# A fused window attention with two gated MLPs on one core: three chunks per output bank, later output weights and integer additions on VectorE in one stage

## The chip, the core and the metric

The kernel runs on one core of a Trainium2 chip. The engines are named as the profile names them: PE (TensorE, the matrix engine; PEld is its weight load), DVE (VectorE), ACT (ScalarE), POOL (GpSimd) and SP (the engine that issues the DMAs here). SBUF is the on-chip memory, PSUM the memory that PE writes its sums to. The metric is the time of one execution on the device, in microseconds; lower is better.

## What is computed

Window attention over four sequences of 576 tokens gives 2304 tokens of 512 numbers. Two gated MLPs follow, each with two input matrices of 512 x 1536 and an output matrix of 1536 x 512. The weights come as float64, and the kernel rebuilds float32 words from them itself. The part that matters here is the second MLP.

```python
x = attn_out.transpose(0, 2, 1, 3).reshape(B * S, H * D)      # 2304 x 512
gate = 1.0 / (1.0 + np.exp(-(x @ w_gate)))                    # first MLP
x = (gate * (x @ w_val)) @ w_out
a = x @ w_a                                                   # second MLP
b = x @ w_b
out = (a * b) @ w_out
```

## The kernel before

**Stages.** Attention comes first and runs on beside the first MLP of tokens 0 to 1279, up to about 341 us of the profiled execution. Then comes the stage of the change, to about 565 us: the second MLP of tokens 256 to 1279. A seam of some 27 us finishes its output and prepares the next operands; after it both MLPs of the last 1024 tokens run to the end.

**A quad.** The hidden width of 1536 is worked off in twelve chunks of 128 (NF = 12). For the 1024 tokens and one chunk, `quad` computes both products with seven matrix products instead of eight (line 846, six matmuls of 512 columns each, in PSUM tiles qa, qb and qc). ACT copies interim sums out (line 865), DVE adds them (line 868) and multiplies a by b (line 878, first qa, at the end qc), and DVE and ACT split the result into a high and a low part (lines 470 and 472). The second half of the hidden values lies in a buffer that `seconds` picks: one of its own, or one of the rings of the weights wa and wb.

**Output banks.** The output rows are eight PSUM banks of 128 x 512 (`row_banks`, `bank_sum`, tile accq, line 984). After every second chunk (PAIR = 2) eight jobs are put into the list `rest`: six matmuls per bank, three for each chunk, and then an addition into an SBUF sum on DVE (line 988); the first group is copied by ACT (line 986). `fill` takes jobs out of the list between the products of later quads. Two PSUM buffers serve these banks. The 256 tokens of block 0 are done on the side for six chunks in this stage (ALONE, `hidden`, line 461, and `projection`, line 514), and for three more in the seam.

**Decoding.** A weight matrix of a chunk (a, b or o for the output) is loaded from HBM into `stage` (three buffers). `decode_words` makes of it: low and ex on ACT (lines 374 and 377), a shift and a mask-and-or on DVE (lines 380 and 383), and the integer addition `wi + low` on POOL (line 387). `decode_pair` multiplies (line 393, DVE), rounds to the high part (line 399, ACT) and subtracts for the low part (line 402: DVE for a and b, POOL for o). Once a and b of a chunk are there, `combining` makes their four combinations, each with two POOL operations and a copy on ACT (lines 439, 441 and 442). The list `order` gives the sequence of the matrices: a, b and o of a chunk, then the next chunk. `need` drives it until a chunk is `ready`, which here happens with its o; `step_decode` takes single steps between the products of a quad. The ring of the output weights wo has four buffers.

**What sets the order.** The program is recorded in this sequence; then a scheduler, which has durations of its own, places the instructions on each engine. Each engine works its list off in order, so an instruction that waits holds up all that stand behind it on that engine.

Of the kernel before, what the change touches and what calls it, by code (L numbers as in the profile page):

```python
# [21 lines left out]
def tile_window_attention_gated_mlps(ctx, tc, q, k, v, w1g, w1v, w1o, w2a, w2b, w2o, out):  # L22
# [346 lines left out]
    def decode_words(F, i, nm):  # L369
        st = staged.pop((F, nm))  # L370
        w0, w1 = st[:, :, 0], st[:, :, 1]
        k = 3 * F + i if F > NF + 2 else 0
# [14 lines left out]
        nc.gpsimd.tensor_tensor(out=wi, in0=wi, in1=low, op=ALU.add)  # L387
# [249 lines left out]
    order = [(F, i, nm) for F in range(DECODED, NW) for i, nm in enumerate("abo")]  # L637
# [3 lines left out]
    def begin_matrix():  # L641
        if begun[0] == 0:
            load_weights(DECODED)
        if begun[0] < len(order):
            F, i, nm = m = order[begun[0]]
            begun[0] += 1
            since = len(nc.cur_bb.bb.instructions)
            whole(decode_words(*m))
            if F == NF + 2 and held[0]:
                for i in nc.cur_bb.bb.instructions[since:]:  # L650
                    tc.add_manual_dep(
                        i, held[0],
                        mybir.DependencyInfo(mybir.DependencyClass.NoSync, mybir.DependencyReason.DATA), reason="held",
                    )
            pending.append(m)
            if F + 1 < NW:
                load_matrix(F + 1, nm)

    def step_decode(turn):
# [17 lines left out]
        if nm == "o":  # L677
            ready[F] = parts[F]
        elif nm == "b" and F >= NF:
            combined_by.append(combining(F))  # L680
        return True
# [9 lines left out]
    def need(F, turn):  # L691
        while F not in ready:
            assert step_decode(turn), (F, turn)
# [409 lines left out]
    def row_banks(res, hs, rows, begin, end):  # L1103
# [3 lines left out]
        for i in range(2 * NP):  # L1107
# [19 lines left out]
    PAIR = 2  # L1127
# [11 lines left out]
    for fc in range(NF):  # L1139
        alone = ALONE.get(fc, ())  # L1140
        for i, f0 in enumerate(alone):
# [4 lines left out]
            if i == len(alone) - 1:  # L1146
                rest.append(lambda a=(1, 0, h0s, fc == 0, False): projection(*a))
# [9 lines left out]
        counts = ((0, 0, 1, 1, 1, 1, 0), (0, 0, 1, 1, 1, 1, 0)) if len(rest) <= 4 else ((0, 1, 1, 1, 1, 1, 1), (0, 1, 1, 1, 1, 1, 1))  # L1157
        extra = max(0, len(rest) - sum(counts[0]))

        def between(i):  # L1160
            fill(counts[0][i] + (extra if i == 4 else 0))
# [3 lines left out]
        hs.append((w["o"], quad(1, w, x_ops, between, g, seconds[fc % 3], lambda: None)))  # L1165
        if len(hs) == PAIR:
            fill(len(rest))
            row_banks(res, hs, (3 * N, N), fc == PAIR - 1, fc == NF - 1)
            hs = []
# [158 lines left out]
```

## Time and profile before

| what | us |
|---|---|
| runs before, median (lowest to highest of 3) | 965.94 (965.51 to 966.07) |
| the profiled execution | 966.96 |
| span of its trace | 965.1 |
| PE busy in the span | 927.0 (96%) |
| DVE busy | 705.4 (73%) |
| ACT busy | 480.0 (50%) |
| POOL busy | 358.7 (37%) |

A busy share is a mean over the whole span. PE is nearly always busy, and the stretches in which it isn't lie in the first 60 us and between 300 and 600 us. What a change in that second part is worth is read from the stretch itself: how long PE stands still there, and for whom.

### The profile page before, as it was taken

What the parts mean: (1) busy time and instruction counts of PE and PEld (TensorE: products, weight loads), DVE (VectorE), ACT (ScalarE), POOL (GpSimd) and SP (SyncE); (2) the same over time, 40 slices, a digit from 0 to 9 for tenths busy, and PEclk for the clock granted to TensorE, in tenths of its full rate; (3) what the DMA queues carried; (4) which work ended last, traced back from release to release, by engine and by line L of the source; (5) the groups of instructions that cost most, each with busy time, mean ns of one, the idle gap of its engine ahead of it and who ended that gap; (6) DMA issues with size and microseconds to landing.
All of it is one profiled execution on the core that took longest, in us unless ns stands there. A gap on an engine that the chain in (4) does not pass through costs nothing.

```text
span 965.1 us, 15642 instructions
## 1 busy us (share of the span) xinstructions
PE 927.0 (96%) x5504; PEld 772.7 (80%) x5504; DVE 705.4 (73%) x1343; ACT 480.0 (50%) x1063; POOL 358.7 (37%) x357
## 2 busy tenths in 40 slices
PE   7899999999999988899999998999999999999998
PEld 6798888888887766787777886788888888888886
DVE  7997877876567899967979576778888673354545
ACT  7887555677635456564645334654454233211111
POOL 4443232343248738855758217644440000000000
PEclk9999999999999999999999999999999999999999
DMA  8987698997478637763765547345456675554312
GB/s 213 247 238 222 217 316 287 336 292 239 138 235 287 218 131 233 257 210 130 251 231 195 196 151 254 117 160 168 135 173 199 217 254 159 167 168 129 102 66 87
DMA packets 144684, 193.68 MB, mean 201 GB/s; under 512 B 63584, under 2 KB 98912, under 8 KB 143968
## 3 DMA queue, kind: packets, MB, share of 16 engines
q1 hardware_dynamic: 144608, 192.71, 61.6%
q8 instruction: 43, 0.70, 0.3%
q14 instruction: 33, 0.27, 0.1%
HBM read 118.75 MB, written 69.47 MB: 195 GB/s over the span
## 4 chain that ended last, share of the span: by engine, by line
PE 48%; DVE 9%; POOL 3%; DMA 3%; issue 2%; ACT 1%; DVEq 0%; POOLq 0%; ACTq 0%
PE qa L846 16%; PE accq L984 11%; PE qb L846 8%; PE qc L846 4%; PE accy L947 3%; PE accx L947 2%; DVE wi L380 1%; DMA st_a<-in_moe_w_a_dram 1%; DVE ex L393 1%; POOL s L439 1%; DVE wi L383 1%; POOL wq L442 1%; PE gps L461 1%; PE vps L461 1%; PE acc L514 1%
## 5 line engine op out<-in xcount | busy, mean ns | idle before, releaser
L387 POOL TENSOR_TENSOR wi<-wi,low 128x512 int32<-128x512 int32 x72 | 103.9, 1443 | 144.2 <-DVE wi L383 109.6
L865 ACT ACTIVATE r<-qa 128x512 f32<-128x512 f32 x108 | 63.6, 596 | 107.6 <-PE qa L846 93.6
L442 POOL TENSOR_TENSOR wq<-s,wq 128x256 fp32r<-128x256 f32 x96 | 86.5, 907 | 73.7 <-ACT wq L441 72.3
L846 PE MATMUL qa<-op,wq 128*128 128x512 f32 x432 | 112.9, 389 | 0.4 <-ACT r L865 0.4
L846 PE MATMUL qb<-op,wq 128*128 128x512 f32 x432 | 111.1, 389 | 0.9 <-DVE qc L868 0.9
L461 PE MATMUL gps<-xh,wa 128*128 128x256 f32 (+1 forms) x392 | 104.9, 338 | 1.5 <-DVE h L472 1.0
L461 PE MATMUL vps<-xh,wb 128*128 128x256 f32 (+1 forms) x392 | 105.3, 337 | 0.8 <-ACT hr L485 0.8
L846 PEld LDWEIGHTS qb<-op,wq 128*128 128x128 f32 x432 | 81.0, 188 | 18.1 <-DVE qc L868 1.3
L846 PEld LDWEIGHTS qa<-op,wq 128*128 128x128 f32 x432 | 80.9, 188 | 17.3 <-ACT r L865 0.6
L562 PE MATMUL accm<-hh,wo 128*128 128x512 f32 (+1 forms) x296 | 87.3, 362 | 3.3 <-DVE gacc L539 1.9
L461 PEld LDWEIGHTS gps<-xh,wa 128*128 128x128 f32 x392 | 68.6, 189 | 11.4 <-DVE h L472 1.5
L461 PEld LDWEIGHTS vps<-xh,wb 128*128 128x128 f32 x392 | 68.9, 189 | 8.7 <-ACT hr L485 1.0
L984 PE MATMUL accq<-wo,h 128*128 128x512 f32 (+1 forms) x300 | 71.7, 382 | 2.8 <-DVE resf L988 2.7
L393 DVE SCALAR_TENSOR_TENSOR ex<-ex,wi 128x512 f32<-128x512 f32 x72 | 59.7, 829 | 17.7 <-POOL wi L387 10.3
L984 PEld LDWEIGHTS accq<-wo,h 128*128 128x128 f32 x300 | 54.9, 188 | 14.9 <-DVE resf L988 3.8
L461 PE MATMUL gps<-xl,wa 128*128 128x256 f32 (+1 forms) x196 | 65.6, 335 | 0.6 <-DVE xl L237 0.6
L470 ACT ACTIVATE hh<-qa 128x512 fp32r<-128x512 f32 x36 | 21.6, 599 | 89.0 <-DVE qa L878 60.0
L461 PE MATMUL vps<-xl,wb 128*128 128x256 f32 (+1 forms) x196 | 65.6, 335 | 0.0
L562 PEld LDWEIGHTS accm<-hh,wo 128*128 128x128 f32 x296 | 54.1, 193 | 13.8 <-DVE gacc L539 4.4
L984 PE MATMUL accq<-wo,hh 128*128 128x512 f32 x184 | 55.7, 394 | 4.9 <-ACT hh L470 3.7
L846 PE MATMUL qa<-op,wa 128*128 128x512 f32 x216 | 55.7, 391 | 3.3 <-DVE g L868 3.3
L846 PE MATMUL qa<-op,wb 128*128 128x512 f32 x216 | 55.3, 391 | 2.4 <-ACT r L865 2.4
(177 smaller groups left out, 2114.9 us busy)
## 6 DMA issues: line engine op xcount, KB each, us to landing
wo<-ko SPq DMA_DIRECT2D x27, 512.0 KB, 3.9
wa<-ka SPq DMA_DIRECT2D x27, 512.0 KB, 4.6
st_o<-in_moe_w_out_dram SPq DMA_DIRECT2D x24, 512.0 KB, 4.9
ka<-wa SPq DMA_DIRECT2D x24, 512.0 KB, 5.1
kb<-wb SPq DMA_DIRECT2D x24, 512.0 KB, 4.1
ko<-wo SPq DMA_DIRECT2D x24, 512.0 KB, 4.0
kq<-wq SPq DMA_DIRECT2D x48, 256.0 KB, 3.2
wq<-kq SPq DMA_DIRECT2D x48, 256.0 KB, 3.2
```

The lines of the kernel that those rows point to most:

```text
L380: nc.vector.tensor_scalar(out=wi, in0=w1, scalar1=3, scalar2=(1 << 30) - 1, op0=ALU.logical_shift_left, op1=ALU.bitwise_and)
L383: nc.vector.scalar_tensor_tensor(out=wi, in0=w1, scalar=-(1 << 30), in1=wi, op0=ALU.bitwise_and, op1=ALU.bitwise_or)
L387: nc.gpsimd.tensor_tensor(out=wi, in0=wi, in1=low, op=ALU.add)
L393: nc.vector.scalar_tensor_tensor(out=wf, in0=wf, scalar=SMALLEST, in1=wi.bitcast(F32), op0=ALU.is_ge, op1=ALU.mult)
L442: nc.gpsimd.tensor_tensor(out=t[:, 1], in0=s, in1=t[:, 0].bitcast(F32), op=ALU.subtract)
L461: nc.tensor.matmul(ps, lhsT=a[:, c * P:(c + 1) * P], rhs=b[:, c, :], start=(n == 0), stop=(n == 3 * NP - 1))
L470: nc.scalar.activation(out=hh, in_=hr, func=AF.Copy, scale=factor)
L562: nc.tensor.matmul(ps[:, m], lhsT=a[:, sl], rhs=b, start=k == 0, stop=k == total - 1)
L846: nc.tensor.matmul(ps, lhsT=a[:, c * P:(c + 1) * P], rhs=b[:, c, :], start=first and n == 0, stop=n == 5, skip_group_check=True,)
L865: nc.scalar.activation(out=r[n], in_=ps, func=AF.Copy)
L947: nc.tensor.matmul(bank[k], lhsT=a[n][i][:, sl], rhs=b[n][j], start=start and m == 0, stop=m == 2, skip_group_check=True,)
L984: nc.tensor.matmul(ps, lhsT=a, rhs=b, start=n == 0, stop=n == len(pairs) - 1)
```

## The change

It has four parts, all in the stage from 341 to 565 us or just ahead of it.

- Output banks are formed after every third chunk (THREE): nine matmuls a bank instead of six, and four groups of eight additions instead of six. `row_banks` takes the banks that use the second halves of the hidden values first (`turned`).
- `order` brings the o of a chunk after the a and b of the next one, from chunk 3 on. A chunk is `ready` with its combinations, and whoever needs the o asks for it by name; loads run three matrices ahead in the same list as before.
- The addition `wi + low` of all matrices of the second MLP is issued on DVE instead of POOL.
- The slots between products take four jobs of the list per quad, whatever its length.

```diff
-        k = 3 * F + i if F > NF + 2 else 0
+        k = order.index((F, i, nm)) if F > NF + 2 else 0
...
-        nc.gpsimd.tensor_tensor(out=wi, in0=wi, in1=low, op=ALU.add)
+        (nc.vector if F >= NF else nc.gpsimd).tensor_tensor(out=wi, in0=wi, in1=low, op=ALU.add)
...
-    order = [(F, i, nm) for F in range(DECODED, NW) for i, nm in enumerate("abo")]
+    order = [(F, i, nm) for F in range(DECODED, NF + 2) for i, nm in enumerate("abo")]
+    for F in range(NF + 2, NW):
+        order += [(F, 0, "a"), (F, 1, "b")] + ([(F - 1, 2, "o")] if F > NF + 2 else [])
+    order.append((NW - 1, 2, "o"))
...
-            if F + 1 < NW:
-                load_matrix(F + 1, nm)
+            if at + 3 < len(order):
+                load_matrix(*order[at + 3][::2])
...
-        if nm == "o":
+        if nm == "o" and F < NF:
             ready[F] = parts[F]
         elif nm == "b" and F >= NF:
             combined_by.append(combining(F))
+            ready[F] = parts[F]
...
-    def need(F, turn):
-        while F not in ready:
+    def need(F, turn, nm="b"):
+        while F not in ready or nm not in parts[F] or nm == "b" and combined_by:
...
-        for i in range(2 * NP):
+        for i in (*range(NP, 2 * NP), *range(NP)) if turned else range(2 * NP):
...
-                rest.append(lambda a=(1, 0, h0s, fc == 0, False): projection(*a))
+                def projected(a=(1, 0, h0s, fc == 0, False), last=NF + f0):
+                    need(last, NEVER, "o")
+                    projection(*a)
+
+                rest.append(projected)
...
-        counts = ((0, 0, 1, 1, 1, 1, 0), (0, 0, 1, 1, 1, 1, 0)) if len(rest) <= 4 else ((0, 1, 1, 1, 1, 1, 1), (0, 1, 1, 1, 1, 1, 1))
-        extra = max(0, len(rest) - sum(counts[0]))
+        counts = (0, 1, 1, 0, 1, 1, 0)
+        extra = max(0, len(rest) - sum(counts)) if len(hs) == THREE - 1 else 0
...
-        if len(hs) == PAIR:
+        if len(hs) == THREE:
             fill(len(rest))
-            row_banks(res, hs, (3 * N, N), fc == PAIR - 1, fc == NF - 1)
+            need(NF + fc, NEVER, "o")
+            row_banks(res, [(w["o"], h) for w, h in hs], (3 * N, N), fc == THREE - 1, fc == NF - 1, True)
```

**Where the instructions stand: DVE in the third quad.** In these rows L487 and L472 with hl belong to block 0, L868, L878 and L472 with h to the quads; L380, L383, L393 and L402 decode. Before, up to the third quad's last multiplication (qc, line 878):

```order
L868 TENSOR_TENSOR g_5225<-qc,r_5236 128x512
L487 TENSOR_TENSOR vps<-vps,hr 128x256
L868 TENSOR_TENSOR qc<-qb,r_5331 128x512
L472 SCALAR_TENSOR_TENSOR hl<-vps,hh 128x256
L878 TENSOR_TENSOR qa<-qa,g_5225 128x512
L472 SCALAR_TENSOR_TENSOR hl<-qa,hh 128x512
L868 TENSOR_TENSOR g_5226<-qb,r_5288 128x512
L878 TENSOR_TENSOR qc<-qc,g_5226 128x512
```

And now, up to the same multiplication (lines moved on by five, so 868 is 873 and 878 is 883):

```order
L873 TENSOR_TENSOR qc<-qb,r_5303 128x512
L472 SCALAR_TENSOR_TENSOR hl<-vps,hh 128x256
L387 ISA wi<-wi,low 128x1024
L393 SCALAR_TENSOR_TENSOR ex<-ex,wi 128x512
L387 ISA wi<-wi,low 128x1024
L380 TENSOR_SCALAR wi<-st_b 128x512
L883 TENSOR_TENSOR qa<-qa,g_5178 128x512
L383 SCALAR_TENSOR_TENSOR wi<-st_b,wi 128x512
L387 ISA wi<-wi,low 128x1024
L472 SCALAR_TENSOR_TENSOR hl<-qa,hh 128x512
L873 TENSOR_TENSOR g_5179<-qb,r_5288 128x512
```

The additions (an instruction of an own kind, ISA, listed with 1024 elements a partition) and decode work that stood elsewhere now stand between the steps of this quad.

**PE at the first output banks.** The names h_4975, h_5109 and h_5325 are the second halves of the first, second and third quad; hh and hl are first halves. Before, where the first bank begins during the second quad:

```order
L846 MATMUL qa<-op_4725,wq_4382 128x512 x6
L846 MATMUL qc<-op_4617,wa 128x512 x6
L984 MATMUL accq<-wo,hh 128x512 x4
L846 MATMUL qa<-op_4613,wa 128x512
L846 MATMUL qa<-op_4614,wa 128x512
```

And now, where the first bank begins, after products of the fourth and fifth quad:

```order
L851 MATMUL qb<-op_4719,wq_5229 128x512
L989 MATMUL accq<-wo,h_4975 128x512 x3
L989 MATMUL accq<-wo,h_5109 128x512 x3
L989 MATMUL accq<-wo,h_4975 128x512 x3
L989 MATMUL accq<-wo,h_5109 128x512 x2
L989 MATMUL accq<-wo,h_5325 128x512 x2
```

The first banks moved behind the third quad, and they begin with eleven matmuls that need only the first two quads.

**DVE in the seam.** L795 (now L800) and L802 (now L807) make the operands of the next stage, L988 (now L993) adds output banks. Before:

```order
L802 TENSOR_TENSOR t_6867<-xq_6824,xq_6820 128x1024
L988 TENSOR_TENSOR resf_4839<-accq,resf_4839 128x512
L795 TENSOR_TENSOR op_6869<-t_6867,op_6869 128x1024
L487 TENSOR_TENSOR vps<-vps,hr 128x256
L988 TENSOR_TENSOR resf_4839<-accq,resf_4839 128x512
L472 SCALAR_TENSOR_TENSOR hl<-vps,hh 128x256
L802 TENSOR_TENSOR t_6905<-xq_6826,t_6867 128x1024
```

Now:

```order
L993 TENSOR_TENSOR resf_4841<-accq,resf_4841 128x512
L993 TENSOR_TENSOR resf_4841<-accq,resf_4841 128x256
L807 TENSOR_TENSOR t_6811<-xq_6768,xq_6764 128x1024
L993 TENSOR_TENSOR resf_4841<-accq,resf_4841 128x256
L993 TENSOR_TENSOR resf_4838<-accq,resf_4838 128x512
L800 TENSOR_TENSOR op_6813<-t_6811,op_6813 128x1024
L487 TENSOR_TENSOR vps<-vps,hr 128x256
```

Each list has the same four differences (L802, now L807) and nine additions in the seam; the additions now come in a row more often.

## Rows read from the trace of the kernel before

**Rows 1.** Stretches: us, PE, PEld, DVE, ACT, POOL busy (x), PEclk, DMA share, GB/s.
```profile
300.00:341.00 41.00, 38.63 (x182) 30.66 (x181) 34.27 (x49) 17.50 (x34) 30.08 (x28) 1.00 0.70 248
341.00:418.00 77.00, 66.08 (x330) 54.22 (x329) 69.49 (x88) 45.98 (x89) 49.96 (x44) 0.98 0.52 179
418.00:565.00 147.00, 141.39 (x640) 116.01 (x638) 116.52 (x167) 72.67 (x136) 82.33 (x79) 1.00 0.58 202
565.00:592.00 27.00, 23.44 (x139) 20.17 (x139) 21.24 (x29) 9.20 (x19) 16.32 (x17) 1.00 0.66 218
```

**Rows 2.** Waits of PE, 418 to 565 us: total us, times, longest.
```profile
PE accq L984 <- DVE resf L988: 1.7, 2, 1.1
PE qa L846 <- DVE g L868: 1.5, 1, 1.5
PE accq L984 <- ACT hh L470: 1.2, 1, 1.2
PE gps L461 <- DVE h L472: 1.0, 1, 1.0
```

**Rows 3.** Waits of PE, 565 to 592 us.
```profile
PE accq L984 <- DVE resf L988: 2.1, 2, 1.7
PE acc L514 <- DVE resf L988: 1.5, 1, 1.5
```

**Rows 4.** Timeline of DVE from 384 us: start, us, what, shapes.
```profile
384.77 0.68 DVE L383 SCALAR_TENSOR_TENSOR wi<-st_b,wi 128x512 int32<-128x512 int32 x1
385.37 1.23 DVE L393 SCALAR_TENSOR_TENSOR ex<-ex,wi 128x512 f32<-128x512 f32 x1
...
387.12 0.41 DVE L380 TENSOR_SCALAR wi<-st_o 128x512 int32<-128x512 int32 x1
```

**Rows 5.** Stretches, DVE busy (x) of lines 380, 383, 393, 402 (then POOL), in turn.
```profile
341.00:418.00 77.00, 9.49 (x11) 0.98 0.52 179
418.00:565.00 147.00, 11.83 (x17) 1.00 0.58 202
...
341.00:418.00 77.00, 11.72 (x11) 0.98 0.52 179
418.00:565.00 147.00, 16.47 (x17) 1.00 0.58 202
...
341.00:418.00 77.00, 11.23 (x10) 0.98 0.52 179
418.00:565.00 147.00, 16.64 (x19) 1.00 0.58 202
...
341.00:418.00 77.00, 6.23 (x6) 2.98 (x2) 0.98 0.52 179
418.00:565.00 147.00, 12.87 (x13) 11.02 (x8) 1.00 0.58 202
```

**Rows 6.** Stretches, POOL busy (x) of line 387.
```profile
341.00:418.00 77.00, 18.80 (x12) 0.98 0.52 179
418.00:565.00 147.00, 25.28 (x17) 1.00 0.58 202
```

**Rows 7.** Groups of DVE, 418 to 592 us: busy, mean ns, idle before.
```profile
L988 DVE TENSOR_TENSOR resf<-accq,resf 128x512 f32<-128x512 f32 (+1 forms) x41 | 26.9, 669 | 10.5 <-PE accq L984 10.5
```

**Rows 8.** Timeline of DVE, last steps of the third quad, idle in brackets.
```profile
411.99 0.70 DVE L878 TENSOR_TENSOR qa<-qa,g 128x512 f32<-128x512 f32 x1 [1.22 <-PE qa L846]
...
416.07 0.69 DVE L868 TENSOR_TENSOR g<-qb,r 128x512 f32<-128x512 f32 x1 [2.02 <-PE qb L846]
416.80 0.70 DVE L878 TENSOR_TENSOR qc<-qc,g 128x512 f32<-128x512 f32 x1
```

**Rows 9.** Chain of work that ended last, at 405 us: start, us, what.
```profile
405.36 2.75 PE accq L984 x12
```

**Rows 10.** Groups of DVE after 592 us: busy, mean ns, idle before.
```profile
L795 DVE TENSOR_TENSOR op<-res,op 128x1024 fp32r<-128x1024 f32 x3 | 3.6, 1216 | 0.0
```

**Rows 11.** Waits, all engines, 418 to 565 us: total us, times, longest.
```profile
POOL wo L402 <- PE accq L984: 1.8, 1, 1.8
```

More of the change, by code (lines that the diff above doesn't have):

```diff
@@ L645, in begin_matrix @@
             F, i, nm = m = order[begun[0]]
+            at = begun[0]
             begun[0] += 1
@@ L1101, in fill, with row_banks @@
             rest.pop(0)()
-    def row_banks(res, hs, rows, begin, end):
+    def row_banks(res, hs, rows, begin, end, turned=False):
         banks = []
-        for i in range(2 * NP):
+        for i in (*range(NP, 2 * NP), *range(NP)) if turned else range(2 * NP):
             j, sl = i // NP, slice(i % NP * P, (i % NP + 1) * P)
@@ L1126, in tile_window_attention_gated_mlps @@
     x_ops = next(built)
-    PAIR = 2
+    PAIR, THREE = 2, 3
     NEVER = 1 << 30
@@ L1156, in tile_window_attention_gated_mlps @@
         g = [tmp.tile([P, W], F32, tag="hr", name=f"g{i}") for i in range(2)]
-        counts = ((0, 0, 1, 1, 1, 1, 0), (0, 0, 1, 1, 1, 1, 0)) if len(rest) <= 4 else ((0, 1, 1, 1, 1, 1, 1), (0, 1, 1, 1, 1, 1, 1))
-        extra = max(0, len(rest) - sum(counts[0]))
+        counts = (0, 1, 1, 0, 1, 1, 0)
+        extra = max(0, len(rest) - sum(counts)) if len(hs) == THREE - 1 else 0
         def between(i):
-            fill(counts[0][i] + (extra if i == 4 else 0))
+            fill(counts[i] + (extra if i == 4 else 0))
             if i != 3:
                 step_decode(NEVER)
-        hs.append((w["o"], quad(1, w, x_ops, between, g, seconds[fc % 3], lambda: None)))
-        if len(hs) == PAIR:
+        hs.append((w, quad(1, w, x_ops, between, g, seconds[fc % 3], lambda: None)))
+        if len(hs) == THREE:
             fill(len(rest))
-            row_banks(res, hs, (3 * N, N), fc == PAIR - 1, fc == NF - 1)
+            need(NF + fc, NEVER, "o")
+            row_banks(res, [(w["o"], h) for w, h in hs], (3 * N, N), fc == THREE - 1, fc == NF - 1, True)
             hs = []
```

## The prediction, made before the changed kernel was run

> **What bounds the kernel now.** I read the table of stretches first, then the waits of PE in each stretch, then the timeline of DVE where PE waits most. PE works 96% of the span, and no matmul is added or removed, so the change can be worth only what PE idles, and where. The stretches tell it [rows 1]. From 300 to 341 us PE idles 41.0 - 38.6 = 2.4 us. From 341 to 418 us it idles 77.0 - 66.1 = 10.9 us, and there DVE is the bound: it works 69.5 of 77 us (that busy time overlaps itself a little: an instruction of 0.68 us starts 0.60 us after the one ahead [rows 4]). From 418 to 565 us PE idles 5.6 us, nearly all of it in four kinds of waits, each behind DVE's list [rows 2]. In the seam, 565 to 592 us, it idles 3.6 us, all for additions of output banks [rows 3]. Together some 22 us; more than that can't be won.
>
> DVE is held up by POOL. Where POOL is idle, a decode instruction with two inputs in SBUF takes 0.68 us and a shift 0.41; next to POOL's work the same kind took 1.23 us [rows 4]. By line [rows 5], with 0.41 us alone for line 380 and 0.68 for the others, the excess from 341 to 418 us is 9.49 - 11 x 0.41 = 5.0, 11.72 - 11 x 0.68 = 4.2, 11.23 - 6.8 = 4.4 and 6.23 - 4.1 = 2.1, in sum 15.7 us over 38 instructions; from 418 to 565 us it is 4.9 + 4.9 + 3.7 + 4.0 = 17.5 us over 66. An addition that reads PSUM shows none of it: 669 ns in the mean of 41 [rows 7].
>
> **The change part by part.** The sum is made against the profiled execution, 966.96 us, with a span of 965.1; the median of the runs is 965.94, 1.02 us below it, and I carry the difference over.
>
> *Integer additions, POOL's side.* Line 387 took 18.8 + 25.3 = 44.1 us [rows 6] of POOL's 49.96 + 82.33 = 132.3 [rows 1], a third. I give it a third of the excess: 5.2 us of relief for DVE in the first stretch and 5.8 in the second. The bounds are none (if DVE then meets the other POOL work instead) and twice that.
>
> *Integer additions, DVE's side.* Before doesn't show this instruction on DVE. Its nearest rows are a decode instruction of 512 elements, 0.68 us alone [rows 4], and, as the listing names 1024 elements, an instruction of that size, 1.22 us [rows 10]. I take 0.68, that is 0.60 from start to start: its data are the same 512 words, and 1024 stands for halves of them. The Trainium skill ("VectorE: DVE Perf Modes", section "What auto-detection actually checks") says that 16-bit operands of unit step run two elements a cycle; by that rule the 1024 halves would cost what 512 words cost, and without it the sum would be that of the first rival below. No run of before shows it. The listing puts 7 additions ahead of 341 us, 12 up to the third quad and 17 behind it. Ahead of 341 us they are 7 x 0.60 = 4.2 us, against 41.0 - 34.3 = 6.7 us in which DVE idles [rows 1]: I take +0.5, with ends 0 and 4.2.
>
> *First three quads.* Up to the third quad's last multiplication DVE's list has 12 instructions more, all of them additions. Each waits like the others once line 387 is off POOL, (15.7 - 5.2) / 38 = 0.28 us: 12 x (0.60 + 0.28) = 10.6 us more and 5.2 less, +5.4. Against it stands idle time of DVE late in this stretch, 1.22 + 2.02 us [rows 8] and, as I estimate, 1.0 in smaller pieces: the multiplication, which ended at 417.5 us [rows 8], comes 1.2 us later. PE has no output banks there now. From the end of the first quad to the third quad's last product its list has 119 matmuls of 512 columns before and 96 now. But it may run ahead: two matmuls of block 0, four products (24) and the 11 bank matmuls that need only the first two quads stand next, 133 in all, by the time the third quad's second half is split, some 2.2 us behind the multiplication. Before was at 126 at 417.5 us and would be at 136 by then. The 3 that are lacking, and 2 that are left over from the first quad, are 5 x 0.23 = 1.1 us [rows 9]. Together +2.3; I keep 0 and 9 as ends (DVE early enough; no relief at all).
>
> *Three chunks per bank, 418 to 565 us.* DVE gets 17 x (0.60 + (17.5 - 5.8) / 66) = 13.2 us of additions, and loses 16 bank additions of 0.60, 9.6 us, and 5.8 us of excess: 2.2 us less in all, beside a POOL with 25 us less to do. Of PE's waits, the 1.7 us for bank additions [rows 2] should go, as a bank now takes 9 x 0.23 = 2.1 us instead of 1.4 and there are half as many; of the other 3.7, behind decode work that POOL held up, I let half go. That is -3.6, with ends +1 and -5.4. DVE has 30 us of idle time there, so its own sum is no bound.
>
> *Output weights a chunk later.* The order of decoding moves with them, and it is in the counts above. SP's loads keep running three matrices ahead of the same list: 0. The o of the next group may wait for the ring until the eight banks are done; the nearest row is 1.8 us on POOL [rows 11], and the same wait on ACT would hold the copies of the quads. I take 0 and keep 1.8.
>
> *Seam.* Nine matmuls a bank instead of six give DVE 2.1 us per addition with the 1.22 us operand work between them [rows 10], so the wait of 2.1 us should go [rows 3]; the wait of 1.5 us by the projection stays and grows, as the last hidden values of block 0 now stand behind the ninth addition: -1.4 with ends -2.5 and +1.
>
> Sum: 0.5 + 2.3 - 3.6 - 1.4 = -2.2 us on the profiled execution, 964.8; less 1.02, **963.8 us**.
>
> **The rivals.** *The addition costs 1.22 us on DVE.* Then 0.54 us more for each: 12 in the stretch where DVE is the bound, +6.5; 17 later, of which a third shows, +3; 7 early, +1.9. In sum -2.2 + 11.4 = +9.2, 975.1. For it speaks the size in the listing, against it the amount of data. It decides from a mean of line 387 on DVE above 1.1 us.
>
> *DVE stays blocked (slower).* POOL's remaining two thirds stand as dense as before in the first three quads, since DVE's list is their clock too, and each addition is one more instruction that meets them; relief is nothing. Then the first three quads cost 5.2 us more, and the additions ahead of them 1: -2.2 + 6.2 = +4.0, 969.9. What speaks for it is that DVE idles only late in this stretch [rows 8], so little there absorbs work; against it, that line 387 has the longest single blocks. It decides if the third quad's multiplication ends later than about 421 us. The Trainium skill ("SBUF — State Buffer", section "Who interferes with whom") has a two-input DVE instruction and a POOL instruction that reads SBUF block each other by turns, whichever came first; by it the moved addition stays in that contest, and only gets shorter in it.
>
> *Waits that move (no change).* The four kinds of waits from 418 to 565 us come from where the scheduler put decode work ahead of urgent DVE work. It places it anew, and other steps may be late: then 2.2 us of the 3.6 are lost, and the time is 966.0.
>
> *More relief (faster).* With POOL's longest operation gone, the other blocks in the first three quads halve too (12 + 38 instructions, 0.28 to 0.2): -4.0 more, 959.8.
>
> **How the numbers follow.** A measurement here tells 0.2%, 1.9 us, from no change. Chances: the forecast 0.34, more relief 0.12, waits that move 0.27, DVE stays blocked 0.20, the dear addition 0.07. Faster by over 0.2% means under 964.0: the forecast's own spread, 961 to 966, lies on both sides of that, and I give 0.26 of its 0.34 to below and 0.08 to above; with more relief and 0.06 of the waits that move that is 0.26 + 0.12 + 0.06 = 0.44. Within 0.2%: 0.08 + 0.21 = 0.29. Slower: 0.20 + 0.07 = 0.27. Cases of both signs hold most of the chance; the likeliest one's own range is 961 to 966. The range that should hold the time 8 times in 10 goes from 958.5 (more relief, and the seam's lower end) to 971.0 (blocked, and the seam's upper end), and leaves out the dear addition and some of each end.
>
> **What would show it.** In the changed profile: line 387 on DVE 36 times with a mean near 0.9 us, and none of them on POOL from 300 us on; 25 bank additions on line 993 instead of 41; the third quad's last multiplication at 417 to 420 us; PE's idle time from 341 to its end about 2 us above 10.9, from there to the seam 2 to 3 us, in the seam 2 us; mean times of lines 380, 383 and 393 down by a tenth to a fifth. Wrong would be the forecast if line 387 means over 1.1 us, if those lines stay as long as they are, if PE waits over 4 us between the fourth quad and the seam, or if anything after the seam changes.

## The result and the profile after

The changed kernel takes 972.72 us (median of 5 runs, 971.13 to 977.81) against 965.94 us before: a ratio of 1.0081, with a 95% interval of 1.0055 to 1.0108. Two more sets of runs gave 1.0045 (1.0029 to 1.0061) and 1.0075 (1.0059 to 1.0092). It is slower, by about 0.7%; the forecast was 0.2% faster. The profiled execution has a span of 970.6 us, 5.5 more than before.

The table of stretches, where [rows 1] stood before (columns: us, PE, PEld, DVE, ACT, POOL busy, granted clock, DMA share, GB/s):

```profile
300.00:341.00 41.00, 38.27 (x185) 30.92 (x184) 36.31 (x55) 18.66 (x37) 25.65 (x25) 1.00 0.71 251
341.00:418.00 77.00, 68.00 (x331) 56.66 (x330) 71.82 (x108) 46.13 (x87) 35.85 (x35) 0.93 0.56 196
418.00:565.00 147.00, 138.41 (x613) 113.07 (x611) 107.69 (x160) 70.70 (x134) 56.37 (x57) 0.98 0.55 191
565.00:592.00 27.00, 25.31 (x150) 21.81 (x150) 16.84 (x23) 8.41 (x17) 15.44 (x19) 1.00 0.63 213
```

PE idles 2.7 + 9.0 + 8.6 + 1.7 = 22.0 us here, before 2.4 + 10.9 + 5.6 + 3.6 = 22.5. By idle time alone nothing is lost. But PE is busy for 932.9 us instead of 927.0 with the same matmuls, and the column of the granted clock says why: 0.93 and 0.98 instead of 0.98 and 1.00. The waits of PE show what stands ahead of that, from 341 to 418 us, then from 418 to 565 us, then behind the seam (total us, times, longest):

```profile
PE qb L851 <- DVE qc L873: 3.0, 1, 3.0
PE vps L461 <- ACT hr L485: 2.9, 1, 2.9
PE gps L461 <- ACT xh L570: 2.2, 1, 2.2
...
PE qa L851 <- DVE g L873: 4.1, 3, 2.4
PE qa L851 <- ACT r L870: 2.6, 2, 2.2
PE qb L851 <- DVE qc L873: 1.7, 1, 1.7
...
PE acc L514 <- DVE resf L993: 1.8, 1, 1.8
```

Before, from 341 to 418 us, the idle time was nine kinds of waits, none longer than 2.1 us. Its two largest rows:

```profile
PE accq L984 <- ACT hh L470: 2.4, 2, 1.3
PE accm L562 <- DVE hl L472: 2.1, 1, 2.1
```

One stretch of the stage ran at a clock of 0.5 then. Now there are a few long waits, and behind six of them, between 340 and 600 us, the clock is granted at 0.5 (1.2 of 2.4 GHz). Two of the six, at 355 and 365 us, are also in the run with the additions alone (below), which is faster than the kernel before. The other four, at 389, 471, 560 and 594 us, are neither there nor in the run with banks of two. The place behind the wait of 2.97 us, in a table of stretches and on PE's timeline (start, us, what, idle before):

```profile
389.50:392.80 3.30, 2.86 (x7) 2.29 (x8) 3.30 (x6) 1.70 (x3) 1.10 (x1) 0.50 0.71 282
471.50:474.70 3.20, 2.99 (x7) 2.41 (x8) 2.88 (x6) 2.89 (x7) 2.14 (x3) 0.50 0.21 82
```
```profile
389.94 2.93 PE L851 MATMUL qb<-op,wq 128*128 128x512 f32 x6 [2.97 <-DVE qc L873]
```

The six matmuls of a product take 2.93 us at the lower clock and 1.52 us at the higher one (below, at 552.43 us).

Since busy time hides this, the rest of the text counts what PE **loses**: the time between two marks less the matmuls in between at their spacing at full clock (0.227 us for 512 columns, 0.12 for 256, from the timelines). It holds idle time and slow matmuls alike. The marks are the last multiplications (qc, line 878 of before) of the 1st, 3rd, 6th, 9th and 12th quad, and the first product behind the seam.

| lost, us | 300 to 1st | to 3rd | to 6th | to 9th | to 12th | seam | 50 us on | sum |
|---|---|---|---|---|---|---|---|---|
| before | 16.3 | 4.4 | 4.4 | 2.6 | 0.6 | 4.7 | 3.1 | 36.1 |
| after | 14.8 | 5.3 | 4.1 | 5.0 | 4.8 | 5.4 | 2.4 | 41.7 |
| additions alone | 15.0 | 3.9 | 2.3 | 2.4 | 0.5 | 4.9 | 2.2 | 31.1 |
| after, banks of two | 16.6 | 3.7 | 0.1 | 3.1 | 0.6 | 4.7 | 2.2 | 31.0 |
| after, two, then three | 15.2 | 4.1 | 0.9 | 4.9 | 1.3 | 3.6 | 2.4 | 32.4 |
| after, last group dealt anew | 15.4 | 5.6 | 3.8 | 5.5 | 1.1 | 4.5 | 2.4 | 38.2 |
| after, early groups dealt anew | 15.3 | 5.6 | 3.9 | 3.7 | 5.0 | 3.8 | 2.4 | 39.7 |
| additions and subtractions | 13.4 | 3.2 | 1.1 | -0.2 | 0.6 | 4.5 | 2.2 | 24.7 |

(The kernels below the second row are the experiments.) From before to after the sum grows by 5.6 us, the span by 5.5. The loss came from quads seven to twelve: 2.4 and 4.2 us.

**What DVE shows.** The additions on DVE from 300 to 592 us (busy, mean ns, idle before):

```profile
L387 DVE CUSTOM_DVE_ANT_0 wi<-wi,low 128x1024 uint16<-128x1024 uint16 x33 | 31.8, 965 | 1.5 <-ACT low L374 0.7
```

And by line, DVE busy in the two stretches, of lines 380, 383, 393 and 402 (then POOL) in turn, which answers [rows 5]:

```profile
341.00:418.00 77.00, 7.49 (x12) 0.93 0.56 196
418.00:565.00 147.00, 9.65 (x16) 0.98 0.55 191
...
341.00:418.00 77.00, 8.54 (x12) 0.93 0.56 196
418.00:565.00 147.00, 12.29 (x17) 0.98 0.55 191
...
341.00:418.00 77.00, 8.05 (x12) 0.93 0.56 196
418.00:565.00 147.00, 14.94 (x18) 0.98 0.55 191
...
341.00:418.00 77.00, 7.06 (x8) 2.83 (x2) 0.93 0.56 196
418.00:565.00 147.00, 9.66 (x11) 11.04 (x8) 0.98 0.55 191
```

With 0.41 us alone for line 380 and 0.68 for the others, the excess is 2.6 + 0.4 - 0.1 + 1.6 = 4.5 us in the first stretch (15.7 before) and 3.1 + 0.7 + 2.7 + 2.2 = 8.7 us in the second (17.5 before). One instruction each of lines 383 and 393 stands across 418 us and is counted in both rows; counted once, the excess is 13.2 + 2 x 0.68 = 14.6 us, 18.6 less than the 33.2 of before. So this part of the change did more good than was forecast (11.0 us), and the loss is elsewhere.

### The profile page after: what moved, and what is told of

Its sections match the earlier page's. It is cut to its first block, busy times and chain, and to the rows that moved or that the text cites. A ratio compares the mean times of both kernels' runs of the same rounds, so it can differ in the third digit from the quotient of the medians.

```text
span 970.6 us, 15635 instructions
## 1 busy us (share of the span) xinstructions
PE 932.9 (96%) x5507; PEld 778.9 (80%) x5507; DVE 701.6 (72%) x1363; ACT 479.2 (49%) x1063; POOL 307.6 (32%) x321
## 4 chain that ended last, share of the span: by engine, by line
PE 71%; DVE 12%; issue 6%; POOL 5%; ACT 4%; DMA 2%; POOLq 0%; DVEq 0%; ACTq 0%
PE qa L851 17%; PE accq L989 11%; PE qb L851 9%; PE vps L461 7%; PE gps L461 7%; PE accm L562 6%; PE qc L851 4%; PE accy L952 3%; PE accx L952 2%; POOL s L439 2%; DVE ex L393 2%; PE xps L228 2%; DVE wi L380 1%; PE acc L514 1%; DVE wi L387 1%
## 5 line engine op out<-in xcount | busy, mean ns | idle before, releaser
L442 POOL TENSOR_TENSOR wq<-s,wq 128x256 fp32r<-128x256 f32 x96 | 84.0, 879 | 106.0 <-ACT wq L441 105.5
L562 PE MATMUL accm<-hh,wo 128*128 128x512 f32 (+1 forms) x296 | 84.8, 356 | 1.8 <-DVE gacc L539 1.8
L387 POOL TENSOR_TENSOR wi<-wi,low 128x512 int32<-128x512 int32 x36 | 50.0, 1388 | 112.3 <-DVE wi L383 74.6
L393 DVE SCALAR_TENSOR_TENSOR ex<-ex,wi 128x512 f32<-128x512 f32 x72 | 54.3, 757 | 16.4 <-ACT ex L377 10.7
L989 PEld LDWEIGHTS accq<-wo,h 128*128 128x128 f32 x303 | 55.0, 188 | 10.9 <-DVE res L993 0.3
L873 DVE TENSOR_TENSOR qc<-qb,r 128x512 f32<-128x512 f32 x36 | 25.0, 695 | 45.3 <-ACT r L870 45.1
```

The source lines that it names most:

```text
L387: (nc.vector if F >= NF else nc.gpsimd).tensor_tensor(out=wi, in0=wi, in1=low, op=ALU.add)
L393: nc.vector.scalar_tensor_tensor(out=wf, in0=wf, scalar=SMALLEST, in1=wi.bitcast(F32), op0=ALU.is_ge, op1=ALU.mult)
L442: nc.gpsimd.tensor_tensor(out=t[:, 1], in0=s, in1=t[:, 0].bitcast(F32), op=ALU.subtract)
L562: nc.tensor.matmul(ps[:, m], lhsT=a[:, sl], rhs=b, start=k == 0, stop=k == total - 1)
L873: nc.vector.tensor_tensor(out=dst, in0=ps, in1=r[n], op=ALU.add)
L989: nc.tensor.matmul(ps, lhsT=a, rhs=b, start=n == 0, stop=n == len(pairs) - 1)
```

## The experiments

Ratios are against the kernel before, in runs on the same chip, with 95% intervals.

### Which part costs

**Additions back on POOL.**

```diff
-        (nc.vector if F >= NF else nc.gpsimd).tensor_tensor(out=wi, in0=wi, in1=low, op=ALU.add)
+        nc.gpsimd.tensor_tensor(out=wi, in0=wi, in1=low, op=ALU.add)
```

> The changed kernel with the integer additions back on POOL; banks of three chunks and late output weights stay. Theory 'bunched banks' (the sixth, ninth and twelfth quad have only 6 to 12 bank matmuls between their products, since the eight jobs of a group go four, four and none, so PE waits there in one piece for DVE and ACT, and each long wait is followed by a stretch at granted clock 0.5): the time stays at 969 to 976 us, waits of over 1.5 us in at least two of these three quads, at least four stretches at clock 0.5 between 340 and 600 us. Rival 'additions on DVE': the time comes back to 964 to 967 us, with no more than two such stretches.

Measured: 972.32 us, 1.0045 (1.0030 to 1.0059). The additions on DVE are not what costs.

**Additions alone**, on the kernel before:

```diff
-        nc.gpsimd.tensor_tensor(out=wi, in0=wi, in1=low, op=ALU.add)
+        (nc.vector if F >= NF else nc.gpsimd).tensor_tensor(out=wi, in0=wi, in1=low, op=ALU.add)
```

> The kernel before with nothing but the integer additions moved to VectorE. Bunched banks: banks of two keep every quad at 24 bank matmuls, so DVE's relief is all that is left: 961 to 965 us, the third quad's last multiplication at 412 to 416 us, PE idle from 418 to 565 us under 5 us, at most two stretches at clock 0.5. Rival 'additions on DVE': 970 us or more, with the waits of the changed kernel between 418 and 565 us. My prediction's own sum for this part alone would be 965 to 970.

Measured: 963.31 us, 0.9949 (0.9933 to 0.9965). PE idles 147.00 - 144.11 = 2.9 us from 418 to 565 us, and the third quad's last multiplication ends at 416.11 us:

```profile
341.00:418.00 77.00, 68.37 (x338) 56.95 (x337) 67.53 (x101) 48.41 (x92) 36.53 (x34) 0.96 0.54 182
418.00:565.00 147.00, 144.11 (x660) 118.39 (x659) 123.93 (x190) 72.18 (x134) 57.35 (x58) 1.00 0.57 201
```

This part alone is a gain of 0.5%. The excess of lines 380, 383, 393 and 402 on DVE is 4.3 us in the first stretch and 9.1 in the second, 19.8 less than before.

**Banks of two again**, with additions on DVE and late output weights (the slots between products and the sequence of the banks are the old ones too):

```diff
-        if len(hs) == THREE:
+        if len(hs) == PAIR:
...
-            row_banks(res, [(w["o"], h) for w, h in hs], (3 * N, N), fc == THREE - 1, fc == NF - 1, True)
+            row_banks(res, [(w["o"], h) for w, h in hs], (3 * N, N), fc == PAIR - 1, fc == NF - 1)
```

> The changed kernel with banks of two chunks in the old sequence and the old slots; additions on DVE and late output weights stay. Bunched banks: 961 to 966 us, no wait of over 2 us after 418 us. Rival 'late output weights' (the changed order of decoding makes PE wait): 970 us or more, with stretches at clock 0.5 after 418 us. If it lies over 1.5 us from the run with the additions alone, the late output weights have a price or a gain of that size.

Measured: 962.92 us, 0.9948 (0.9932 to 0.9963), the same as the additions alone. So the late output weights cost nothing and bring nothing, and banks of three, with their slots and their sequence, cost 1.0045 to 1.0081 against 0.9948, 9 to 13 us. The sequence (`turned`) was not tried apart.

### How banks of three cost it

The eight jobs of a group are taken four in the next quad and four in the one behind, so the third has none. By the traces, between the last product of one quad and that of the next, from the fourth quad on, PE has 12, 36, 18, 18, 24, 24, 24, 24 and 27 bank matmuls before, and now 36, 36, 12, 6, 36, 30, 6, 36 and 24. My first theory was that this bunching costs.

**Jobs dealt out three, three and two.**

```diff
-            fill(2)
+            fill(1 if fc == 4 else 2)
...
-        counts = (0, 1, 1, 0, 1, 1, 0)
-        extra = max(0, len(rest) - sum(counts)) if len(hs) == THREE - 1 else 0
+        number = -(-len(rest) // (THREE - len(hs)))
+        counts = {2: (0, 0, 0, 0, 1, 1, 0), 3: (0, 0, 1, 0, 1, 1, 0)}.get(number, (0, 1, 1, 0, 1, 1, 0))
+        extra = max(0, number - sum(counts))
```

> The changed kernel with the eight jobs of a group dealt out three, three and two to the quads that follow instead of four, four and none; nothing else is changed. Bunched banks: 966 to 970 us, PE idle from 418 to 565 us 2 to 4 us below the 8.6 us of the changed kernel, one to three stretches at clock 0.5 fewer. Both rivals (additions on DVE, late output weights): no change, 971 to 974 us.

Measured: 969.13 us, 1.0017 (1.0004 to 1.0030). The gain is the one expected, but not where it was: the waits near 470 and 517 us stay (2.51 and 2.87 us on PE's timeline), and of the long ones only that near 558 us falls, to 0.74 us. That spoke against the theory; the last sections show why.

**Banks of two for six chunks, then of three.**

```diff
+        size = PAIR if fc < 6 else THREE
...
-        if len(hs) == THREE:
+        if len(hs) == size:
...
```

(the last six chunks with the dealing of the run before, the first six with the old sequence of the banks)

> The changed kernel with banks of two chunks for the first three groups and banks of three for the last six chunks, whose jobs are dealt out three, three and two. Theory 'no bank work in the first three quads and bunched work later': 962 to 966 us; the wait near 387 us under 2 us, the one near 469 us gone, what is left of long waits lies in the ninth and tenth quad. Rival 'a bank of nine matmuls is itself the trouble': 968 us or more, with the waits between 500 and 565 us as long as with banks of three everywhere. If it equals banks of two everywhere (962.9 us in the set before), the last two groups are free in either size.

Measured: 966.09 us, 0.9982 (0.9967 to 0.9996). The wait near 469 us is gone (0.9 instead of 3.8 to 4.1 us lost up to the sixth quad), the one near 518 us is still 2.56 us. The wait near 390 us, where I expected under 2 us, is 2.0. Banks of three cost where they are.

**The changed kernel again**, as a base for the runs beside it:

> The changed kernel once more, on the chip of the three runs beside it. All theories: 1.003 to 1.011 of the kernel before. If the ratio comes out at 1.003 to 1.006, the additions on DVE have no price beside banks of three chunks; if at 1.008 or more, they have one there though they bring 0.5% beside banks of two.

Measured: 972.95 us, 1.0045 (1.0029 to 1.0061). With 1.0081 and 1.0075 in the other two sets it can't be told from the run with the additions back on POOL: beside banks of three the additions bring nothing that can be measured, beside banks of two they bring 0.5%.

### Does the clock cost by itself?

**Useless matmuls in two of the waits.** Eight stand ahead of product 3 of the second quad and six ahead of product 4 of the twelfth, where an output bank also moves in front of that product.

```diff
...
+        ps = ps_acc.tile([P, W], F32, tag="acc", name="warmq")
+        for m in range(n):
+            nc.tensor.matmul(ps, lhsT=w["a"][0][:, 0:P], rhs=w["a"][0], start=m == 0, stop=m == n - 1)
...
```

> The changed kernel with useless matmuls of 512 columns on PE in two of its long waits: eight ahead of product 3 of the second quad (the wait of 2.97 us near 387 us) and six ahead of product 4 of the twelfth (the wait of 2.22 us near 558 us, where one output bank also moves in front of it). Their results are read by nobody. Theory 'the clock answers the long wait': the granted clock stays at 1.0 behind both places, the six matmuls of each product take 1.5 us instead of 2.9, and the time is 3 to 5 us under that of the changed kernel in this same set. Rival 'the waits themselves are the loss' (the clock costs nothing of its own): the waits are only filled, the product starts no earlier, the time is the same within 1.5 us or longer by what does not fit into the waits.

Measured: 975.41 us, 1.0071 (1.0055 to 1.0087), 2.5 us over the changed kernel of this set. The clock did stay at 1.0 behind both places. PE's timeline at the first:

```profile
390.04 1.97 PE L866 MATMUL warmq<-wa 128*128 128x512 f32 x8
393.19 1.66 PE L851 MATMUL qb<-op,wq 128*128 128x512 f32 x6 [1.17 <-DVE qc L904]
...
398.75 0.39 PE L461 MATMUL gps<-xh,wa 128*128 128x256 f32 x1 [2.54 <-DVE hl L472]
```

Product 3 takes 1.66 us instead of 2.93, and then PE waits 2.54 us for DVE, where it didn't wait in the changed kernel. Against the changed kernel of this set, the way from the first quad's mark to the third's is 33.55 instead of 34.57 us, and from the ninth's to the twelfth's (with the bank that moved) 41.86 instead of 43.24; from the third's to the sixth's and in the seam it is 1.0 and 2.6 us longer. The forecast of 3 to 5 us fell. But the total says little about the clock: in the profiled execution PE's matmuls start 1.8 us later from 53 us on, in code that is the same, and the first quad's mark, ahead of both places, is 3.6 us later (383.43 instead of 379.78 us). The Trainium skill ("TensorE: Matmul & The Clock Gate", section "HAM oscillation — how this bites in real kernels") counts the time at the low clock as a penalty in wall time. An estimate by its rule, from the rows (2.93 - 1.52 = 1.4 us on each product), is 2.8 us for the two stretches; at their places 1.0 and 1.4 us came back, and the time of the run shows none of it. How much of a slow stretch is lost again in the next wait for DVE stays open.

### Is DVE still late?

**Subtractions for o on DVE too**, on the kernel with the additions alone:

```diff
-        engine = nc.gpsimd if F >= NF and nm == "o" else nc.vector
-        engine.tensor_tensor(out=wl, in0=wf, in1=wh.bitcast(F32), op=ALU.subtract)
+        nc.vector.tensor_tensor(out=wl, in0=wf, in1=wh.bitcast(F32), op=ALU.subtract)
```

> The kernel before with the integer additions and also the subtraction of the output weights' low part (line 402 for o) moved from POOL to DVE. Theory 'relief goes on' (each operation taken from POOL shortens more on DVE than it adds): 957 to 962 us, lines 380, 383 and 393 within 10% of their times alone from 341 to 418 us. Rival 'DVE is full': 963 to 967 us, the third quad's last multiplication 1 to 3 us later than with the additions alone (416.1 us).

Measured: 957.55 us, 0.9880 (0.9862 to 0.9898), the fastest of all by its ratio. PE idles 147.00 - 146.28 = 0.7 us from 418 to 565 us:

```profile
418.00:565.00 147.00, 146.28 (x694) 122.40 (x693) 124.88 (x200) 70.81 (x132) 53.73 (x52) 1.00 0.60 213
```

The relief goes on, though not as far as expected: from 341 to 418 us lines 380 and 383 are still 18% and 15% above their times alone.

**The same with banks of three** (the edit above on the changed kernel):

> The changed kernel with the subtraction of the output weights' low part (line 402 for o) on DVE too, as in the run that brought 957.6 us with banks of two. It asks whether the price of banks of three, about 9 to 10 us beside the additions alone (972.9 against 963), depends on how late DVE is. Theory 'PE waits for a late DVE wherever it has no bank work': with DVE relieved the price falls to 6 us or less, 958 to 963 us. Rival 'the bunching costs the same whatever DVE does': 965 to 969 us.

Measured: 973.72 us, 1.0076 (1.0055 to 1.0098). Both sides of the expectation fell, as both had it faster: the price of banks of three rose to 16 us by the medians (19 by the ratios). The waits for DVE near 470 us did shrink, from 2.4 to 0.9 us, so that wait is DVE's; but the loss from the ninth to the twelfth quad grew to 6.6 us, and PE waits there for ACT.

**The same with the jobs dealt out three, three and two:**

> The same with the eight jobs of a group dealt out three, three and two. Theory: with bank work in each quad from the fourth on and DVE relieved, banks of three cost at most 4 us against banks of two with the same work on DVE (957.6 us): 956 to 961 us, what is left being the first three quads, which have no bank work. Rival 'a bank of nine matmuls is itself the trouble': 963 us or more.

Measured: 969.70 us, 1.0021 (1.0011 to 1.0032), the same as without the subtractions on DVE. This is the rival's side of the expectation.

**Line 439 on DVE too**, on banks of two:

```diff
-            nc.gpsimd.tensor_tensor(out=s, in0=x, in1=y, op=op)
+            nc.vector.tensor_tensor(out=s, in0=x, in1=y, op=op)
```

> The kernel before with the integer additions, the subtraction for o and the first operation of each combination (line 439, 128x256, about 1.0 us on POOL) on DVE. Theory 'relief goes on': each costs DVE some 0.35 us and takes a block of about 1 us away: 950 to 956 us. Rival 'DVE is full by now': 957 to 962 us, the third quad's last multiplication later than the 413.5 us of the run with the subtractions.

Measured: 960.55 us, 0.9931 (0.9918 to 0.9945). Neither side: the time is the rival's, a smaller gain than with the subtractions alone, but the third quad's last multiplication is earlier (408.6 us) and not later.

**Lines 439 and 442 both on DVE:**

> The kernel before with all of POOL's work of the second MLP's weights on DVE: line 387, line 402 for o, lines 439 and 442. Theory 'relief goes on': with no POOL work left in the stage every DVE instruction takes its time alone (0.41 and 0.68 us), which outweighs some 96 more instructions of 0.35 us: 948 to 955 us. Rival 'DVE is full by now': 958 us or more, PE idle from 341 to 418 us above the 6.8 us of the run with the subtractions.

Measured: 956.60 us, 0.9896 (0.9881 to 0.9912), no better than the subtractions, and between the two sides of the expectation. Here DVE's instructions take their time alone (excess 0.5 and 0.6 us in the two stretches), and little is lost up to the seam (10.1, 1.4, -0.1, 0.0 and 0.1 us), but from 592 to 700 us, where the combinations are made again, PE idles 3.5 us instead of 0.8.

### The twelfth quad

In the changed kernel PE's wait of 2.22 us near 558 us is for ACT's copy of product 7 (line 870). ACT's timeline shows what is ahead of it:

```profile
554.49 1.05 ACT L799 ACTIVATE op<-xq 128x1024 fp32r<-128x1024 f32 x1
558.66 1.06 ACT L799 ACTIVATE op<-xq 128x1024 fp32r<-128x1024 f32 x1 [3.12 <-DMA xq<-bx]
559.62 0.58 ACT L870 ACTIVATE r<-qa 128x512 f32<-128x512 f32 x1
```

An operand copy for the next stage (line 799) waits for a load, and the quad's copy stands behind it. The loads on SP's queue, after and then before:

```profile
540.16 0.80 SPq L1188 DMA_DIRECT2D xq<-bx  x2
552.17 0.32 SPq L832 DMA_DIRECT2D wo<-ko  x1
552.63 0.34 SPq L1188 DMA_DIRECT2D xq<-bx  x1
...
553.50 0.42 SPq L1188 DMA_DIRECT2D xq<-bx  x1
```
```profile
542.62 3.72 SPq L1178 DMA_DIRECT2D xq<-bx  x4
```

The last one is issued at 553.5 us instead of about 546. Ahead of it stands a load of output weights that waited 11.1 us for its ring. That was the second theory.

**The base once more:**

> The changed kernel in the set of the two runs beside it, as their base. All theories: 1.003 to 1.010 of the kernel before, with a wait of PE for ACT's copy of 2.2 to 2.4 us near 558 us.

Measured: 974.04 us, 1.0075 (1.0059 to 1.0092).

**The four loads ahead on SP's queue:**

```diff
+    operand_load = next(reversed(nc.cur_bb.bb.instructions)).name
...
+    for load in nc.cur_bb.bb.instructions[tied:]:
+        if load.engine == mybir.EngineType.SP:
+            tc.add_manual_dep(
+                load, operand_load,
+                mybir.DependencyInfo(mybir.DependencyClass.NoSync, mybir.DependencyReason.DATA), reason="loads",
+            )
```

> The changed kernel with the four loads of the next operands (line 1188) ahead of the load of output weights (line 832) on SP's queue; the lists of PE, DVE and ACT are the same. Theory 'the queue of SP': the loads are issued before 547 us as in the kernel before, ACT's operand copy waits under 1 us for them, PE's wait of 2.2 us before product 4 of the twelfth quad and the stretch at clock 0.5 behind it are gone: 2.5 to 4 us faster than the changed kernel of this set. Rival 'bunched bank work': that wait stays above 1.5 us and the time within 1.5 us of it.

Measured: 974.31 us, 1.0080 (1.0068 to 1.0092). No change, and the loads are as late as before (from 541.03 us, over 13.04 us):

```profile
541.03 13.04 SPq L1188 DMA_DIRECT2D xq<-bx  x4
```

So it isn't the queue. With nothing ahead of them, the queue's own waits show what the last two loads wait for (us, times, longest), a product in qb on PE:

```profile
SPq L1188 <- PE qb L851: 11.6, 1, 11.6
```

**The same with the subtractions on DVE:**

> The same edit on the kernel with banks of three and line 402 for o on DVE (973.7 us in its set, 1.0076 of the kernel before), which waits 3.4 us at that place. Theory 'the queue of SP': 3.5 to 6 us faster than 1.0076, that is 1.0015 to 1.004. Rival: 1.006 or more. What then still lies above the 0.988 of banks of two with the same work on DVE is another cause, to be read from the waits before 550 us.

Measured: 974.13 us, 1.0072 (1.0052 to 1.0092), no change either.

The loads wait for something of their own. Their buffers (`quarter`) are those of operands 1 and 5 of this stage, and product 5 of the twelfth quad, in qb, reads operand 5. The chain of work that ended last in the changed kernel runs through them (start, us, what), and behind it stand two products on PE's timeline and the wait:

```profile
548.06 4.08 PE accq L989 x18
552.14 0.47 PE qb L851 x2
552.63 5.95 DMA xq<-bx
```
```profile
552.43 1.52 PE L851 MATMUL qa<-op,wq 128*128 128x512 f32 x6
...
556.51 1.52 PE L851 MATMUL qa<-op,wq 128*128 128x512 f32 x6
560.26 2.93 PE L851 MATMUL qa<-op,wb 128*128 128x512 f32 x6 [2.22 <-ACT r L870]
```

The two at 552.14 us are the last of that product. They stand behind 18 bank matmuls, two banks of nine, and the load starts right behind them.

**The last group alone dealt out three, three and two** (the edit of that run, only for chunks 9 to 11):

> The changed kernel with the jobs of the last group alone (quads ten to twelve) dealt out three, three and two; up to the tenth quad nothing moves. Theory 'the operand buffer' (the last load of the next operands waits for product 5 of the twelfth quad, whose last matmuls stand behind two banks of nine; ACT's copy for the quad stands behind the operand copy that waits for the load): the last load is issued at least 3 us earlier, PE's wait of 2.2 to 2.4 us near 558 us falls under 1 us, no stretch at clock 0.5 there, and the time is 2.5 to 4 us under the changed kernel, 1.003 to 1.005 of the kernel before. Rival 'bunched bank work in all groups': 1.006 or more.

Measured: 970.17 us, 1.0022 (1.0009 to 1.0036). The four loads are now issued within 8.96 us from 540.99 us on, so the last some 4 us earlier, and the wait falls to 0.7 us, with the clock at 1.0 behind it:

```profile
540.99 8.96 SPq L1190 DMA_DIRECT2D xq<-bx  x4
```
```profile
SPq L1190 <- PE qb L851: 7.5, 1, 7.5
...
PE qa L851 <- ACT r L870: 0.7, 1, 0.7
```

**The groups before it alone dealt anew:**

> The changed kernel with the jobs of the groups before the last dealt out three, three and two, and the last group as it is. Theory 'the operand buffer' plus a smaller part for bunched work: the wait near 558 us and its stretch at clock 0.5 stay, 0 to 2 us faster than the changed kernel, 1.005 to 1.008. Rival 'bunched bank work': 1.003 to 1.0045, with the waits near 470 and 516 us under 1.5 us.

Measured: 972.21 us, 1.0056 (1.0033 to 1.0080). The wait near 559 us stays, at 2.6 us, and so do those near 470 and 520 us. The last group's dealing holds the whole gain of the first dealing run (1.0017 and 1.0022), and dealing the other groups anew is not shown to gain anything.

### The sixth quad

What is left is the waits for DVE. DVE's timeline ahead of PE's wait of 2.38 us near 469 us:

```profile
465.98 1.12 DVE L393 SCALAR_TENSOR_TENSOR ex<-ex,wi 128x512 f32<-128x512 f32 x1
467.02 1.22 DVE L387 CUSTOM_DVE_ANT_0 wi<-wi,low 128x1024 uint16<-128x1024 uint16 x1
468.16 0.96 DVE L380 TENSOR_SCALAR wi<-st_b 128x512 int32<-128x512 int32 x1
469.16 0.69 DVE L383 SCALAR_TENSOR_TENSOR wi<-st_b,wi 128x512 int32<-128x512 int32 x1
469.77 0.69 DVE L883 TENSOR_TENSOR qa<-qa,g 128x512 f32<-128x512 f32 x1
470.37 0.68 DVE L387 CUSTOM_DVE_ANT_0 wi<-wi,low 128x1024 uint16<-128x1024 uint16 x1
470.97 0.68 DVE L873 TENSOR_TENSOR g<-qb,r 128x512 f32<-128x512 f32 x1
```

Decode work, three of its instructions stretched by POOL, stands ahead of the multiplication and of the addition to g for which PE waits, and in these microseconds PE has no bank left to work on. With the subtractions off POOL the same wait is 0.9 us, and with banks of two it is gone.

PE's timelines show the gap itself, from the last product of a quad to the first of the next. Behind the sixth quad PE has 10 and 7 bank matmuls there with banks of two (additions alone; additions and late weights) and waits 0.54 and 0 us; it has none in the changed kernel and one with the jobs dealt anew, and waits 2.38 and 2.51 us. So the dealing had not filled this gap, and the wait stayed. The kernel of two, then three, holds both cases: behind the sixth quad nine bank matmuls and no wait, behind the ninth none and this:

```profile
520.49 1.65 PE L851 MATMUL qa<-op,wa 128*128 128x512 f32 x6 [2.56 <-DVE g L873]
```

Whether a bank put into these gaps of the changed kernel, or another order on DVE, would cure it was not tried.

## Why the prediction was wrong, point by point

**The additions: right on DVE, too small on POOL.** I took 0.68 us for an addition alone; 19 of the 36 take 0.68 to 0.73 us, the others up to 1.78 next to POOL, and the mean of those from 300 us on is 0.965. The first rival (1.22 us each) fell. The relief was mis-sized: I gave line 387 a third of the excess, 11.0 us; the excess fell by 18.6 of 33.2 us, and by 19.8 with the additions alone. PE idles 9.0 us from 341 to 418 us, where I had 13.2. That is the side of the rival "more relief", and the rival "DVE stays blocked" fell: its mark was 421 us. The third quad's last multiplication came at 413.55 us, 4.0 us earlier, where I had it 1.2 us later, but little of that is relief: it comes at 414.58 us with the additions back on POOL, at 416.11 with the additions alone and at 417.51 with banks of two. The first quad's mark was 5.3 us earlier already, and from there to the third's the way is 1.3 us longer than before. One reading was wrong and did no harm: [rows 4] has an instruction of 0.68 us at 384.77 us, and I took POOL to be idle there, but its line 442 began at the same time. That 0.68 us is the time alone is shown by the kernel with all this work off POOL. Alone, the additions give 0.9949, about 961 us on the median of before; my sum for them had no gain of that size.

**Output weights a chunk later: right.** Priced at nothing; 0.9948 with them and 0.9949 without.

**Three chunks per bank: the step that failed.** I wrote -3.6 us, with +1 as the worst end; measured, this part costs 9 to 13 us. I had it as a gain because the 1.7 us of waits for bank additions should go and half of the others with them. The first happened: no wait for line 993 is left between 418 and 565 us. But the banks were also the work that covers a quad's own chain, product, copy on ACT, addition on DVE. Now the sixth, seventh and tenth quad have 12, 6 and 6 of their matmuls, where they had 18, 18 and 24, and the gaps behind the sixth and the ninth have none. New waits came, 4.1 + 2.6 + 1.7 us, twice the 4 us that I had named as a sign of being wrong, with stretches at the lower clock behind two of them. The one ahead of the sixth quad's mark takes the place of what before lost there (4.1 and 4.4 us; 2.3 with the additions alone); from that mark to the twelfth's the loss grows by 6.6 us. I had taken the length of PE's list into account at one place only, the first three quads, where I priced lacking work at 1.1 us. Of the 6.6 us, some 4 are the twelfth quad's chain from two banks to an operand buffer, a load, ACT's list and PE: I had said of SP that its loads keep their distance, and looked at their order but not at the buffers that they wait for.

**The rival "waits that move"** had the mechanism (the scheduler places the work anew, and other steps are late), but I priced it as a gain that is lost, 2.2 of 3.6 us. Nothing in the rows of before bounded it there: a wait that moves can be longer than the one that it replaces.

**The clock had no term.** [rows 1] showed 0.98 in the stretch where PE waits longest. One stretch of the stage at the lower clock became six. The run with the useless matmuls leaves open how much of that is a cost beside the waits, but idle time alone, which I summed, was no measure: it is the same before and after.

**The seam: not gained.** PE idles 1.7 instead of 3.6 us up to 592 us, as forecast; but the wait for the projection's bank, which I had let grow, is 1.8 us and lies just behind 592 us, with a slow stretch after it. From mark to mark the seam loses 5.4 us instead of 4.7.

The range ended at 971.0 us. The terms that were left out, together some 10 us against the same kernel with banks of two, were outside of it.

## What to carry to other kernels

Work that looks like a burden of its own (here the output banks with their waits) may be the cover for another chain's latency: before making it rarer, look at what PE would do in each gap without it, and at which buffers its new place keeps busy, down to the loads that wait for them. Count a stage by the time between marks less its matmuls at full speed, since neither idle nor busy time alone shows a loss that is part waiting and part low clock. And take a change of several parts apart: with the additions and the subtractions on DVE and the banks left alone the kernel runs at 0.9880.

## What the runs showed of the hardware that was not expected

An addition of 512 integer words a partition on DVE, listed as 1024 16-bit elements, takes 0.68 us alone, as a 512-element instruction does. This is what the Trainium skill ("VectorE: DVE Perf Modes", section "What auto-detection actually checks") would give, and the rows agree.

Taking one of POOL's lines away (44.1 of 132.3 us of its busy time) took 19.8 of the 33.2 us away by which DVE's decode instructions were stretched (the run with the additions alone), though the additions themselves now stand in DVE's list. The next step, 10 subtractions of 1.4 us, brought another 0.7%.

Behind waits of PE of 2.19, 2.92, 2.97, 2.38 and 2.22 us the granted clock was 0.5; behind those of 1.73 and 1.40 us at 516 and 521 us it stayed at 1.0. Behind the one of 1.79 us in the seam, with waits of 0.6 and 0.4 us just ahead of it, it was 0.5. The length of a wait alone doesn't tell: with the jobs dealt out three, three and two the clock stayed at 1.0 behind waits of 2.21 and 2.87 us, at 352 and 519 us.
